# A Fourier filter with two MLPs on one core: the third matrix's sums, loads, spare buffers and output stores are re-timed

## The chip, the core and the metric

The kernel runs on one core of one Trainium2 chip. The metric is device time in microseconds (us) of one execution; times are compared by the median of several executions. TensorE (PE) multiplies matrices, VectorE (DVE) and ScalarE (ACT) work on tiles element by element, GpSimd (POOL) does a little arithmetic and issues the accumulating transfers, SyncE (SP) issues most other transfers. Each engine runs its instructions in order and waits on semaphores of the others.

## The reference

The input is two batches of 3008 tokens by 256 features. It is filtered along the tokens in the frequency domain, and the 6016 tokens then go through two MLPs, all in float32:

```
X = np.fft.rfft(x, axis=1)
y = np.fft.irfft(X * (filt_r + 1j * filt_i)[None], n=3008, axis=1)   # 2 x 3008 x 256
h = y.reshape(6016, 256) @ w_in              # 256 -> 2048
x2 = (h * sigmoid(h)) @ w_out                # 2048 -> 256
g = x2 @ w_gate                              # 256 -> 1536
out = (g * sigmoid(g) * (x2 @ w_val)) @ w_out2   # 1536 -> 256
```

## The kernel before

The filter is a prime-factor transform of 64 by 47 points done with matrix products. Numbers are split in a high and a low part, both of a type that TensorE takes, and a product of two such operands is three matmuls (high by high, high by low, low by high). Where "operand" stands below, making one means a copy by ScalarE that rounds to the high part and a subtraction by VectorE that leaves the low part.

Three stages follow one another on TensorE: the filter, the first MLP (its last blocks as `Wide` units) and the second MLP, from about 604 us to the end. Only that last stage and its seam with the stage before matter here. It works on 6 blocks of up to 1024 tokens (`STEP2`), 6 units of `Pair` per block, 36 in all. A unit computes a part of gate and value (`Gate`, g and v) by a scheme with 7 products of quarter blocks in the place of 8, so 14 products or 42 matmuls, and leaves SiLU(g) times v in two tiles: ga (L1026, with both quarters of one row of the scheme) and c.

**Gate and value on the side engines.** In a unit ScalarE copies banks of sums on (L876, L879, L894) and applies SiLU (L1027, L1031, L1037, L1039), VectorE adds banks (L903, L909) and multiplies by the values (L1045, L1049, L999, L1008). TensorE's next products wait for L876, L894 and L909, which put back into PSUM what it goes on accumulating.

**The third matrix** (w_out2) is multiplied by the same scheme on pairs of units: 17 "chains" (`CHAINS`) of two units each, 3 per block, with the last unit pair done by 16 plain products (`product8`). The chains run beside the units on the same engines. `Pair.run` calls `tick()` (L1208) seven times; each tick may queue one product of three matmuls (`product7`), which TensorE then does between those of gate and value. The clock starts at tick −19, and a chain takes 14 ticks: seven operands k in the order 3, 1, 7, 5, 2, 6, 4 (`ORDER7`), each for its pair-halves p = 0 and 1 (the two units). Around a chain's tick 0 stand, by tables of tick numbers:

- `high7` (L1097) and `lower7` (L1102) make operand k, so many ticks ahead of its product (`EARLY`).
- `more` (L1086 to 1090) makes the sums that some operands are, in place: `SUMS` names the tick, the target k and the addend j. The first, (1, 7), adds two quarters in ga, to be operand 5; (1, 3) and (7, 3) add a quarter of c to ga, (4, 6) one of ga to c. A sum is a transfer of POOL's queue that adds as it writes (L1088), 256 KB; in the first and the last two chains the first sum is VectorE's (L1090).
- `load7` (L1108 to 1111) has SP load the third matrix's parts in four pieces, up to 512 KB each, into tiles w7 of the pool `late["p"]`, 9 buffers that ga, w7 and the input differences xr share in turn.
- `after7` (L1123, L1125, L1136, L1142) adds the products' banks into oa, and `store2` turns an oa tile (L1250) and writes it out by 4 strided transfers per quarter on SP (L1253).

**What is in between.** `side(k)` runs what a table (`todo2`, filled by `later`) holds for a step of a unit: the loads of gate and value weights (`load_s2`), the next block's input x2 (`load_x2`), its differences on POOL (`prep_x2`, L809) and its operands xo (`split_x2`; L796 on ScalarE, L799 on VectorE). `split_op` can put the low half on a list `lag` for later. The order of every engine is that of the program text; buffers of a pool are handed out in turn, and a tile waits until its buffer's last reader is done.

**The seam.** In the first MLP's last block ScalarE copies four x2 tiles from the sums (L748) and issues their stores itself (L750). The spare pool here called sp has 2 buffers of the tag s, for `Gate.s` of the `Wide` units and `done7` of the chains; the pool tp has 4 of the tag u.

Of the kernel before, what the change touches and what calls it, by code (L numbers as in the profile page):

```python
# [11 lines left out]
F32 = mybir.dt.float32  # L12
# [17 lines left out]
P = 128  # L30
# [3 lines left out]
STEP2 = 1024  # L34
# [85 lines left out]
def fft_filter_mlp_kernel(  # L120
# [609 lines left out]
    def wide_out(b, f, h):  # L730
# [5 lines left out]
        def one(m, l, k):  # L736
# [9 lines left out]
            if end and k == 1:  # L746
                u = tp.tile([P, 512], F32, tag="u", name="x2")
                nc.scalar.copy(u[:, :n], a)  # L748
                eng = nc.scalar if b == len(WIDE) - 1 else nc.sync
                eng.dma_start(d3[NSTD + 2 * b + l][:, m, :n], u[:, :n])  # L750
# [56 lines left out]
    def prep_x2(t, part):  # L807
# [6 lines left out]
        if t:  # L814
            r = late["p"].tile([P, 2, 512], F32, tag="mid", name="xr")
        else:
            r = mid([P, 2, 512], "xr")
# [267 lines left out]
    def more(c, k, j, p):  # L1085
        o, v = view(c, k, p), view(c, j, p)  # L1086
        if (k, j) != (1, 7) or 0 < c < CHAINS - 2:
# [4 lines left out]
    SUMS = ((-5, 1, 7), (1, 1, 3), (4, 7, 3), (8, 4, 6))  # L1092

    def high7(c, k, p):
        x = ops7[c, k, p] = mid([P, 2, 512], "ho", F32R)
# [69 lines left out]
    for p, first in ((0, (-9, -8, -7, -6)), (1, (-4, -3, -2, -1))):  # L1165
# [24 lines left out]
    def product8(p, v, l, m, i):  # L1190
# [10 lines left out]
        if end and i == 2:  # L1201
            a = turned[t, m][:, l, :n]
            nc.vector.tensor_tensor(a, o, a, op=ALU.add)
            if l == 1:
                turned["o", m] = mid([P, 2, 512], "ob")
            store2_part(t, m, l, turned[t, m], turned["o", m], (nc.sync, nc.scalar))

    def tick():  # L1208
# [13 lines left out]
        for k in ORDER7:  # L1222
            at7 = where(i + EARLY[k] - 1, k)
            if at7:
                lower7(*at7)
        for k in ORDER7:
            at7 = where(i + EARLY[k], k)
            if at7:
                high7(*at7)
        for o, k, j in SUMS:  # L1230
            c, r = divmod(i - o, 14)
            if r < 2 and 0 <= c < CHAINS:
                more(c, k, j, r)
        for r, o in enumerate((-4, 3, 9, 21)):
# [6 lines left out]
    def store2(t, m):  # L1241

        o = mid([P, 2, 512], "ob")
        a = turned.pop((t, m))
        for l in range(2):
            store2_part(t, m, l, a, o)

    def store2_part(t, m, l, a, o, engines=(nc.sync,)):
        n = size2(t) // 2
        nc.vector.transpose(o[:, l, :n], a[:, l, :n])  # L1250
        r0 = STEP2 * t + n * l
        for i in range(4):
            engines[i % len(engines)].dma_start(  # L1253
                out[r0:r0 + n, P * m + 32 * i:P * m + 32 * i + 32].rearrange("(j r) c -> r j c", r=32),
                o[32 * i:32 * i + 32, l, :n].rearrange("p (j c) -> p j c", c=32),
# [105 lines left out]
    for u in range(6 * NBLK2):  # L1361
        later(u, 0, load_s2, u + 1, "g")
# [3 lines left out]
    for t in range(1, NBLK2):  # L1366
        for m in range(2):
            later(6 * t + 3 + 2 * m, 2 - m, store2, t - 1, m)
# [3 lines left out]
        for k, n in ((0, 1), (1, 5), (3, 6)):  # L1372
            later(u + 4, k, split_x2, t, n)
# [278 lines left out]
```

## Time and profile before

| what | value |
|---|---|
| median of 3 executions | 1156.52 us (1152.58 to 1157.79) |
| the profiled execution | 1157.94 us, its span 1156.2 us |
| mean granted clock of TensorE | 0.989 |
| TensorE, VectorE, ScalarE, POOL busy | 97%, 72%, 67%, 35% |
| TensorE's share of the chain of waits | 82% (transfers 6%, VectorE 5%, ScalarE 5%) |
| DMA | 215.62 MB, 48.4% of 16 engines' time by the hardware queues, 17.2% by POOL's |

The span is what the profiler saw between the first and the last instruction; the execution's own time is 1.74 us longer, and the median of the three is 1.42 us shorter than this execution. "Busy" is a share of the whole span. The profile names lines of the kernel: L843 is the matmul of gate and value (and of all second-matrix-like products), L1150 that of a chain. A matmul of 128 by 512 starts some 0.23 us after the one before where nothing is in its way.

### The profile page before, as it was taken

To read this page: it belongs to the slowest core of one execution; us is meant where nothing else is said; L and a number is where in the kernel's file an instruction comes from. 1 tells how busy PE (TensorE), PEld (TensorE's weight loads), DVE (VectorE), ACT (ScalarE), POOL (GpSimd) and SP (SyncE) were. 2 spreads that over 40 slices of the span, in tenths; PEclk is the share of its full clock that TensorE was granted. 3 is DMA by queue.
4 is the path that set the end of the run, shared out by engine and by line. 5 is a ranking of instruction groups with operands and counts; after the bars stand their busy time and mean duration, and the time that the engine had idled before them with its cause. 6 is when DMAs were issued, how large, how long until landed. Compare 5 with 4: busy or idle time off the path is not lost.

```text
span 1156.2 us, 15345 instructions
## 1 busy us (share of the span) xinstructions
PE 1116.5 (97%) x4999; PEld 917.0 (79%) x4999; DVE 835.4 (72%) x1297; ACT 774.0 (67%) x1461; POOL 407.8 (35%) x382
## 2 busy tenths in 40 slices
PE   9999999999999999999999999999998999998996
PEld 7588888998888887888877788778777777877886
DVE  5987365666676786776646788787796786876885
ACT  5788766766677686686556776666675676675671
POOL 3557735554513542632102333222322322322120
PEclk9999999999999999999999999999998999998998
DMA  8974543337355356435446788798899789789794
GB/s 240 287 239 110 158 134 113 128 116 227 109 178 169 136 195 212 147 134 195 170 173 204 157 222 233 172 266 237 191 218 232 166 216 270 165 210 236 180 234 82
DMA packets 148815, 215.62 MB, mean 186 GB/s; under 512 B 58880, under 2 KB 87936, under 8 KB 148736
## 3 DMA queue, kind: packets, MB, share of 16 engines
q1 hardware_dynamic: 125280, 179.26, 48.4%
q0 software_dynamic: 18720, 33.69, 17.2%
q10 hardware_dynamic: 4736, 1.70, 0.6%
q8 instruction: 39, 0.64, 0.2%
q14 instruction: 40, 0.33, 0.1%
HBM read 138.20 MB, written 42.73 MB: 156 GB/s over the span
## 4 chain that ended last, share of the span: by engine, by line
PE 82%; DMA 6%; DVE 5%; ACT 5%; issue 2%; SPq 0%; ACTq 0%; DVEq 0%
PE bk L843 21%; PE acc L742 15%; PE bk L1150 11%; PE acc L719 7%; PE h L669 7%; PE y L843 6%; DMA ga<-ga 4%; PE xb L843 4%; PE xa L843 4%; PE s L209 2%; PE s L397 2%; PE s L206 2%; DMA w<-d 1%; PE s L282 1%; ACT ho L1097 1%
## 5 line engine op out<-in xcount | busy, mean ns | idle before, releaser
L843 PE MATMUL bk<-xo,wst 128*128 128x512 f32 (+1 forms) x864 | 281.6, 391 | 20.1 <-ACT bk L876 15.1
L742 PE MATMUL acc<-h,w 128*128 128x512 f32 x768 | 283.6, 389 | 0.0
L1150 PE MATMUL bk<-ho,w 128*128 128x512 f32 (+1 forms) x714 | 269.1, 394 | 0.2 <-DMA w<-d 0.2
L843 PE MATMUL bk<-xo,w 128*128 128x512 f32 (+1 forms) x648 | 211.1, 392 | 7.7 <-DVE c L909 7.2
L843 PEld LDWEIGHTS bk<-xo,wst 128*128 128x128 f32 x864 | 163.4, 190 | 58.5 <-ACT bk L876 19.2
L742 PEld LDWEIGHTS acc<-h,w 128*128 128x128 f32 x768 | 144.2, 188 | 29.6
L1150 PEld LDWEIGHTS bk<-ho,w 128*128 128x128 f32 x714 | 137.3, 192 | 25.2 <-DMA w<-d 0.5
L843 PEld LDWEIGHTS bk<-xo,w 128*128 128x128 f32 x648 | 121.2, 189 | 39.4 <-DVE c L909 15.9
L1088 POOL DMA_DIRECT2D ga<-c x68 | 59.5, 1086 | 244.7 <-DVE ho L1102 210.1
L1097 ACT CAST ho<-ga 128x512 fp32r<-128x512 f32 (+1 forms) x136 | 82.6, 619 | 30.1 <-DMA ga<-ga 28.6
L1102 DVE TENSOR_TENSOR ho<-ga,ho 128x512 fp32r<-128x512 f32 (+1 forms) x136 | 90.8, 675 | 8.4 <-ACT ho L1097 8.4
L719 PE MATMUL acc<-h,w 128*128 128x512 f32 (+1 forms) x384 | 95.4, 376 | 0.0
L669 PE MATMUL h<-xh,w 128*128 128x512 f32 (+1 forms) x248 | 83.6, 379 | 0.0
L719 PEld LDWEIGHTS acc<-h,w 128*128 128x128 f32 x384 | 71.2, 188 | 11.2
L1102 DVE TENSOR_TENSOR ho<-c,ho 128x512 fp32r<-128x512 f32 (+1 forms) x102 | 77.1, 758 | 1.4 <-ACT ho L1097 1.4
L677 DVE TENSOR_TENSOR h<-h,h 128x512 fp32r<-128x512 f32 (+1 forms) x64 | 41.4, 654 | 48.3 <-ACT h L676 46.9
L843 PE MATMUL xb<-xo,wst 128*128 128x512 f32 x192 | 74.7, 391 | 1.6 <-DVE h L936 1.6
L843 PE MATMUL xa<-xo,w 128*128 128x512 f32 x192 | 75.3, 394 | 0.0
L843 PE MATMUL y<-xo,wst 128*128 128x512 f32 x192 | 74.7, 389 | 0.0
L876 ACT COPY bk<-bk 128x512 f32<-128x512 f32 (+1 forms) x72 | 41.2, 572 | 48.7 <-PE bk L843 24.8
L903 DVE TENSOR_TENSOR bk<-bk,u 128x512 f32<-128x512 f32 (+1 forms) x72 | 49.2, 684 | 27.5 <-PE bk L843 23.2
L1088 POOL DMA_DIRECT2D ga<-ga x28 | 24.1, 860 | 114.0 <-DVE ho L1102 55.1
(161 smaller groups left out, 2208.9 us busy)
## 6 DMA issues: line engine op xcount, KB each, us to landing
w<-d SPq DMA_DIRECT2D x53, 512.0 KB, 6.9
wst<-ds_g SPq DMA_DIRECT2D x36, 512.0 KB, 5.7
wst<-ds_v SPq DMA_DIRECT2D x36, 512.0 KB, 5.3
wst<-ds SPq DMA_DIRECT2D x32, 512.0 KB, 4.6
ga<-c POOLq DMA_DIRECT2D x60, 256.0 KB, 4.6
c<-ga POOLq DMA_DIRECT2D x30, 256.0 KB, 5.7
ga<-ga POOLq DMA_DIRECT2D x28, 256.0 KB, 7.6
zt<-d SPq DMA_DIRECT2D x16, 384.0 KB, 4.7
```

What stands on the lines that cost most here:

```text
L206: nc.tensor.matmul(o, cst[:k, c:c + n], x, start=True, stop=True)
L669: nc.tensor.matmul(ps[:, :n], wt[key, f // 4, g][:, wpart, o:o + P], x[xpart][:, g, :n], start=(g == 0 and k == 0), stop=(g == 1 and k == 2),)
L677: nc.vector.tensor_tensor(h[:, 1, :n], u[:, :n], h[:, 0, :n], op=ALU.subtract)
L719: nc.tensor.matmul(a[:, :n], w[:, wpart, o:o + 128], h[:, xpart, :n], start=(f == 0 and k == 0), stop=(f == 15 and k == 2),)
L742: nc.tensor.matmul(a, w[:, wpart, o:o + 128], h[xpart][:, n * l:n * l + n], start=(f == 0 and k == 0), stop=(end and k == 1), skip_group_c ...
L843: nc.tensor.matmul(o, w(wpart), x[:, xpart, :o.shape[-1]], start=(first and k == 0), stop=(last and k == 2), skip_group_check=True,)
L876: nc.scalar.copy(self.y, self.a)
L903: nc.vector.tensor_tensor(self.b, self.b, self.u2, op=ALU.add)
L1088: nc.gpsimd.dma_start(o, v, accum_op=ALU.add)
L1097: nc.scalar.copy(x[:, 0, :v.shape[-1]], v)
L1102: nc.vector.tensor_tensor(x[:, 1, :n], v, x[:, 0, :n], op=ALU.subtract)
L1150: nc.tensor.matmul(o, w7[c, k][:, p, wpart], ops7[c, k, p][:, xpart, :n], start=(k in (1, 5) and p == 0 and i == 0), stop=(k in (2, 3, 4) ...
```

## The change

Seven edits. TensorE's matmuls and their order stay as they are.

1. In the first MLP's last block two of the four x2 copies go to VectorE, and all four stores to POOL's queue.
2. The input differences of `prep_x2` go into a spare buffer of sp (tag s) in place of one of `late["p"]` (of `mid` for the first block).
3. The first sum: pair-half 0 by POOL's transfer at tick −7 (from −5), pair-half 1 always by VectorE at tick −4. `SUMS` now has a tick for each pair-half. Operand 1's copy of pair-half 0 is made 3 ticks sooner, into a tile of `late["p"]`.
4. The first load of a chain at tick −2 (from −4), the gate weights' load one side step later.
5. The last block's extra operands (`HIGH8`) at ticks −4 to −1 and 2 to 5 after chain 16 (from −9 to −6 and −4 to −1).
6. `store2` by quarters, at four places of a block where two halves stood; the turned tile is from tp.
7. The low halves of the next block's operands are put off to the next `side()` call, and `prep_x2`'s second part comes one step later.

```diff
--- before.py
+++ after.py
@@ -745,8 +745,8 @@
             )
             if end and k == 1:
                 u = tp.tile([P, 512], F32, tag="u", name="x2")
-                nc.scalar.copy(u[:, :n], a)
-                eng = nc.scalar if b == len(WIDE) - 1 else nc.sync
+                (nc.vector.tensor_copy if m and b == len(WIDE) - 1 else nc.scalar.copy)(u[:, :n], a)
+                eng = nc.gpsimd if b == len(WIDE) - 1 else nc.sync
                 eng.dma_start(d3[NSTD + 2 * b + l][:, m, :n], u[:, :n])
 
         queue.extend((one, m, l, k) for m in range(2) for k in (0, 2) for l in range(2))
@@ -811,10 +811,7 @@
             x[4] = x[2]
             sub(x[4], x[2], x[6])
             return
-        if t:
-            r = late["p"].tile([P, 2, 512], F32, tag="mid", name="xr")
-        else:
-            r = mid([P, 2, 512], "xr")
+        r = sp.tile([P, 2, STEP2 // 2], F32, name="s")
         x[5], x[6], x[7] = x["b12"], r[:, 1, :n], r[:, 0, :n]
         sub(x[7], x[3], x["b12"])
         sub(x[5], x["b12"], x[1])
@@ -1084,15 +1081,19 @@
 
     def more(c, k, j, p):
         o, v = view(c, k, p), view(c, j, p)
-        if (k, j) != (1, 7) or 0 < c < CHAINS - 2:
+        if (k, j, p) != (1, 7, 1):
             nc.gpsimd.dma_start(o, v, accum_op=ALU.add)
         else:
             nc.vector.tensor_tensor(o, o, v, op=ALU.add)
 
-    SUMS = ((-5, 1, 7), (1, 1, 3), (4, 7, 3), (8, 4, 6))
+    SUMS = (((-7, -4), 1, 7), ((1, 2), 1, 3), ((4, 5), 7, 3), ((8, 9), 4, 6))
 
     def high7(c, k, p):
-        x = ops7[c, k, p] = mid([P, 2, 512], "ho", F32R)
+        if (k, p) == (1, 0):
+            x = late["p"].tile([P, 2, 512], F32R, tag="mid", name="ho")
+        else:
+            x = mid([P, 2, 512], "ho", F32R)
+        ops7[c, k, p] = x
         v = view(c, k, p)
         nc.scalar.copy(x[:, 0, :v.shape[-1]], v)
 
@@ -1162,7 +1163,7 @@
             for m in range(2):
                 AT8[T0 + first[2 * x + m]] = p, v, l, m
     HIGH8 = {}
-    for p, first in ((0, (-9, -8, -7, -6)), (1, (-4, -3, -2, -1))):
+    for p, first in ((0, (-4, -3, -2, -1)), (1, (2, 3, 4, 5))):
         for x, (v, l) in enumerate(((0, 0), (0, 1), (1, 1), (1, 0))):
             HIGH8[T0 + first[x]] = p, v, l
 
@@ -1201,9 +1202,7 @@
         if end and i == 2:
             a = turned[t, m][:, l, :n]
             nc.vector.tensor_tensor(a, o, a, op=ALU.add)
-            if l == 1:
-                turned["o", m] = mid([P, 2, 512], "ob")
-            store2_part(t, m, l, turned[t, m], turned["o", m], (nc.sync, nc.scalar))
+            store2(t, m, l, (nc.sync, nc.scalar))
 
     def tick():
         i = clock[0]
@@ -1219,40 +1218,34 @@
         at7 = where(i)
         if at7:
             queue.extend((product7, *at7, k) for k in range(3))
-        for k in ORDER7:
-            at7 = where(i + EARLY[k] - 1, k)
-            if at7:
-                lower7(*at7)
-        for k in ORDER7:
-            at7 = where(i + EARLY[k], k)
-            if at7:
-                high7(*at7)
-        for o, k, j in SUMS:
-            c, r = divmod(i - o, 14)
-            if r < 2 and 0 <= c < CHAINS:
-                more(c, k, j, r)
-        for r, o in enumerate((-4, 3, 9, 21)):
+        for d, fn in ((1, lower7), (0, high7)):
+            for k in ORDER7:
+                for p in range(2):
+                    at7 = where(i + EARLY[k] + 3 * (k == 1 and p == 0) - d, k)
+                    if at7 and at7[2] == p:
+                        fn(*at7)
+        for when, k, j in SUMS:
+            for p in range(2):
+                c, r = divmod(i - when[p], 14)
+                if r == 0 and 0 <= c < CHAINS:
+                    more(c, k, j, p)
+        for r, o in enumerate((-2, 3, 9, 21)):
             c, x = divmod(i - o, 14)
             if x == 0 and 0 <= c < CHAINS:
                 load7(c, r)
 
     turned = {}
 
-    def store2(t, m):
-
-        o = mid([P, 2, 512], "ob")
-        a = turned.pop((t, m))
-        for l in range(2):
-            store2_part(t, m, l, a, o)
-
-    def store2_part(t, m, l, a, o, engines=(nc.sync,)):
+    def store2(t, m, l, engines=(nc.sync,)):
+
         n = size2(t) // 2
-        nc.vector.transpose(o[:, l, :n], a[:, l, :n])
+        o = tp.tile([P, 512], F32, tag="u", name="ob")
+        nc.vector.transpose(o[:, :n], turned[t, m][:, l, :n])
         r0 = STEP2 * t + n * l
         for i in range(4):
             engines[i % len(engines)].dma_start(
                 out[r0:r0 + n, P * m + 32 * i:P * m + 32 * i + 32].rearrange("(j r) c -> r j c", r=32),
-                o[32 * i:32 * i + 32, l, :n].rearrange("p (j c) -> p j c", c=32),
+                o[32 * i:32 * i + 32, :n].rearrange("p (j c) -> p j c", c=32),
             )
 
 
@@ -1359,24 +1352,24 @@
         for n, args in enumerate((("g", q), ("v", q), ("a22", q))):
             later(2 * q - 2, n, load_2, *args)
     for u in range(6 * NBLK2):
-        later(u, 0, load_s2, u + 1, "g")
+        later(u, 1, load_s2, u + 1, "g")
         later(u, 3, load_s2, u + 1, "v")
     later(0, -1, split_x2, 0, 7)
     later(0, 0, split_x2, 0, 4)
     for t in range(1, NBLK2):
-        for m in range(2):
-            later(6 * t + 3 + 2 * m, 2 - m, store2, t - 1, m)
+        for n, k, m, l in ((3, 2, 0, 0), (4, 0, 0, 1), (4, 2, 1, 1), (5, 0, 1, 0)):
+            later(6 * t + n, k, store2, t - 1, m, l)
         u = 6 * t - 6
         later(u + 2, 0, load_x2, t)
         later(u + 3, 1, prep_x2, t, 0)
         for k, n in ((0, 1), (1, 5), (3, 6)):
-            later(u + 4, k, split_x2, t, n)
+            later(u + 4, k, split_x2, t, n, True)
 
         for k, n in ((1, 2), (4, 3)):
-            later(u + 5, k, split_x2, t, n)
-        later(u + 5, 2, prep_x2, t, 1)
-        later(u + 6, -1, split_x2, t, 7)
-        later(u + 6, 0, split_x2, t, 4)
+            later(u + 5, k, split_x2, t, n, True)
+        later(u + 5, 3, prep_x2, t, 1)
+        later(u + 6, -1, split_x2, t, 7, True)
+        later(u + 6, 0, split_x2, t, 4, True)
 
 
     F0, F1 = Fft(0), Fft(1)
@@ -1598,6 +1591,9 @@
         for u in range(6 * NBLK2):
 
             def side(k):
+                now, lag[:] = lag[:], []
+                for fn in now:
+                    fn()
                 for fn, args in todo2.pop((u, k), ()):
                     fn(*args)
```

The changed file is shorter by 3 lines from L818 on; L1097 becomes L1098, L1102 L1103, L1111 L1112, L1150 L1151, and of the lines above the chains L876 becomes L873, L894 L891, L903 L900, L909 L906, L1027 L1024, L1031 L1028, L1088 L1085, L1090 L1087, L1250 L1243, L1253 L1246.

On POOL, two chains of the second block. ga<-ga is a first sum, c<-ga the (4, 6) sum, ga<-c the sums with a quarter of c; L809 works on the next block's differences. Before:

```order
L1088 DMA c<-ga 128x512
L1088 DMA ga<-ga 128x512
L1088 DMA c<-ga 128x512
L1088 DMA ga<-ga 128x512
L1088 DMA ga<-c 128x512 x4
L809 TENSOR_TENSOR x_5781<-x_5781,xr 128x512
```

And in the changed kernel:

```order
L1085 DMA ga<-ga 128x512
L1085 DMA c<-ga 128x512 x2
L1085 DMA ga<-c 128x512 x4
L809 TENSOR_TENSOR x_5779<-x_5779,s 128x512
L1085 DMA ga<-ga 128x512
L1085 DMA c<-ga 128x512 x2
```

One first sum per chain is left on POOL, and it stands ahead of both (4, 6) sums of the chain before.

On VectorE, the place in the first block where the next block's operands are made (L799; xo<-x and xo<-xr, later xo<-s). Before:

```order
L903 TENSOR_TENSOR bk<-bk,u_5997 128x512
L1102 TENSOR_TENSOR ho<-c,ho 128x512
L909 TENSOR_TENSOR c<-bk,s_5977 128x512
L799 TENSOR_TENSOR xo<-x_5780,xo 128x512
L1102 TENSOR_TENSOR ho<-c,ho 128x512
L1102 TENSOR_TENSOR ho<-ga,ho 128x512
L799 TENSOR_TENSOR xo<-xr,xo 128x512
L1045 SCALAR_TENSOR_TENSOR ga<-bk,ga 128x512
L1102 TENSOR_TENSOR ho<-ga,ho 128x512
L903 TENSOR_TENSOR bk<-bk,u_6062 128x512
L1049 TENSOR_TENSOR ga<-bk,ga 128x512
L909 TENSOR_TENSOR c<-bk,s_6049 128x512
```

And in the changed kernel:

```order
L1087 TENSOR_TENSOR ga<-ga 128x512
L900 TENSOR_TENSOR bk<-bk,u_5997 128x512
L1103 TENSOR_TENSOR ho<-c,ho 128x512
L906 TENSOR_TENSOR c<-bk,s_5979 128x512
...
L900 TENSOR_TENSOR bk<-bk,u_6062 128x512
L1046 TENSOR_TENSOR ga<-bk,ga 128x512
L906 TENSOR_TENSOR c<-bk,s_6048 128x512
L996 SCALAR_TENSOR_TENSOR c<-c 128x512
L1103 TENSOR_TENSOR ho<-ga,ho 128x512
L799 TENSOR_TENSOR xo<-s,xo 128x512
```

The low half xo<-xr stood ahead of the sums L903 and L909 of its step; xo<-s stands behind them. The row L1087 is an added first sum of pair-half 1.

On SP, the loads of a chain in the second block (w_ is a w7 tile, wst gate or value weights). Before:

```order
L1111 DMA w_6531<-d_0_109 128x1024
L648 DMA wst<-ds_v_103 128x1024
L648 DMA wst<-ds_g_98 128x1024
L1111 DMA w_6651<-d_0_109 128x1024
L1253 DMA out_dram<-ob 32x16x32 x8
```

And in the changed kernel:

```order
L648 DMA wst<-ds_g_97 128x1024
L1112 DMA w_6556<-d_0_109 128x1024
L648 DMA wst<-ds_v_103 128x1024
L1112 DMA w_6649<-d_0_109 128x1024
L648 DMA wst<-ds_g_98 128x1024
L1246 DMA out_dram<-ob 32x16x32 x4
```

The chain's first load (from d_0) keeps its neighbours and is released two ticks later; the output goes four strips at a time.

## Rows read from the trace of the kernel before

**Rows 1.** The page, first part: busy us, share of the span, instructions

```profile
PE 1116.5 (97%) x4999; PEld 917.0 (79%) x4999; DVE 835.4 (72%) x1297; ACT 774.0 (67%) x1461; POOL 407.8 (35%) x382
```

**Rows 2.** TensorE's waits from 603 us on: total us, times, longest us

```profile
PE bk L843 <- ACT bk L876: 15.1, 10, 3.5
PE bk L843 <- DVE c L909: 7.2, 6, 2.0
PE bk L843 <- ACT ga L1027: 2.7, 4, 0.7
PE bk L843 <- ACT u L894: 2.3, 1, 2.3
```

**Rows 3.** TensorE's timeline: start us, us, what; in brackets the idle time ahead

```profile
779.09 0.50 PE L843 MATMUL bk<-xo,wst 128*128 128x512 f32 x1 [2.12 <-ACT bk L876]
...
872.20 0.80 PE L843 MATMUL bk<-xo,wst 128*128 128x512 f32 x1 [3.40 <-ACT bk L876]
...
966.58 0.80 PE L843 MATMUL bk<-xo,wst 128*128 128x512 f32 x1 [2.06 <-ACT bk L876]
...
1060.30 0.74 PE L843 MATMUL bk<-xo,wst 128*128 128x448 f32 x1 [3.55 <-ACT bk L876]
...
1128.91 0.68 PE L843 MATMUL bk<-xo,w 128*128 128x448 f32 x2 [1.98 <-DVE c L909]
```

**Rows 4.** ScalarE's timeline at 773 to 782 us

```profile
777.94 0.62 ACT L1097 CAST ho<-ga 128x512 fp32r<-128x512 f32 x1 [3.74 <-DMA ga<-ga]
778.46 0.58 ACT L876 COPY bk<-bk 128x512 f32<-128x512 f32 x1
```

**Rows 5.** The chain of waits from 590 us on: start us, us, what

```profile
767.52 10.40 DMA ga<-ga
...
859.33 11.68 DMA ga<-ga
...
955.07 10.34 DMA ga<-ga
```

**Rows 6.** Groups by line from 603 us on, ScalarE: busy us, mean ns, idle before

```profile
L1097 ACT CAST ho<-ga 128x512 fp32r<-128x512 f32 (+1 forms) x136 | 82.6, 619 | 30.1 <-DMA ga<-ga 28.6 <-DMA ga<-c 1.3
```

**Rows 7.** Timelines of ScalarE and VectorE at 734 to 747 us

```profile
735.71 0.60 ACT L1027 ACTIVATE ga<-bk 128x512 f32<-128x512 f32 x1 [1.97 <-PE bk L1150]
...
742.39 0.69 DVE L799 TENSOR_TENSOR xo<-xr,xo 128x512 fp32r<-128x512 f32 x1 [2.64 <-ACT xo L796]
```

**Rows 8.** Windows: us, busy of PE, PEld, DVE, ACT, POOL, PE's clock, DMA, GB/s

```profile
850.00:900.00 50.00, 46.60 (x193) 37.73 (x193) 35.60 (x58) 30.16 (x57) 9.57 (x11) 0.93 0.94 235
950.00:975.00 25.00, 22.94 (x94) 18.31 (x93) 17.74 (x29) 15.41 (x30) 6.30 (x8) 0.93 1.01 262
1025.00:1050.00 25.00, 23.97 (x108) 19.60 (x107) 23.97 (x40) 17.31 (x34) 8.39 (x9) 1.00 0.86 206
1050.00:1075.00 25.00, 21.45 (x90) 18.44 (x89) 14.56 (x25) 13.29 (x27) 5.21 (x6) 0.86 0.90 234
```

**Rows 9.** Groups by line from 603 us on, VectorE's first sums

```profile
L1090 DVE TENSOR_TENSOR ga<-ga 128x448 f32<-128x448 f32 (+1 forms) x6 | 3.9, 647 | 0.2
```

**Rows 10.** ScalarE's timeline at the stage's opening

```profile
603.82 0.58 ACT L748 COPY x<-acc 128x512 f32<-128x512 f32 x1 [0.45 <-ACT x L748]
604.44 0.33 ACTq L750 DMA_DIRECT2D d<-x  x1
```

**Rows 11.** The page, DMA issues: queue, count, KB each, median us to landing

```profile
w<-d SPq DMA_DIRECT2D x53, 512.0 KB, 6.9
...
ga<-c POOLq DMA_DIRECT2D x60, 256.0 KB, 4.6
...
ga<-ga POOLq DMA_DIRECT2D x28, 256.0 KB, 7.6
```

**Rows 12.** DMA issues at 732.6 to 733.2 us

```profile
w<-d SPq DMA_DIRECT2D x1, 512.0 KB, 11.6
```

## The prediction

> **What bounds the kernel now.** I began with the page: TensorE is busy 1116.5 us of the span, 97% [rows 1]. The reader should see that only what makes TensorE wait, or slows its clock, can be won. The change leaves TensorE's own instructions and their order as they are, so the question is which of its waits go and which come.
>
> Second, the waits of TensorE from 603 us on, the stage that the change rearranges: 15.1 us on ScalarE's copies at L876 (10 waits), 7.2 on VectorE's sums at L909 (6), 2.7 on ScalarE's L1027 (4), 2.3 on L894 (1) [rows 2], 27.3 us together. Third, TensorE's timeline, to place them. The four longest waits on L876 are 2.12, 3.40, 2.06 and 3.55 us, ending at 779.09, 872.20, 966.58 and 1060.30 us [rows 3], one per block of the stage: 11.13 us. That leaves 4.0 us of L876's; and 1.98 of L909's is one wait near the end, at 1128.91 [rows 3].
>
> *Why the four long ones.* ScalarE reached its copy L1097 of a first sum at 774.2 us and stood still 3.74 us until a transfer ga<-ga was in at 777.94; L876, which TensorE needed, is the next instruction on ScalarE and came at 778.46 [rows 4]. In the chain of waits that transfer runs from 767.52 for 10.40 us, and its fellows in the other blocks take 10.34 to 11.68 us (four rows, the shortest and longest shown) [rows 5]. Over the stage ScalarE idles 28.6 us for ga<-ga at L1097, and 1.3 us for ga<-c [rows 6].
>
> *Why the rest.* At 735.71 ScalarE's L1027 has waited 1.97 us for TensorE's third-matrix product L1150: its new tile takes a buffer of which a product still reads weights. ScalarE is then late with its copies, and VectorE idles 2.64 us for ScalarE's xo before L799, an operand's low half, with L909 queued behind it [rows 7]. Such a group stands in each of four blocks; it and two waits at the stage's opening make up 4.0 + (7.2 − 1.98) + 2.7 = 11.9 us of TensorE's waits [rows 2, 3].
>
> The low clock is the last item. The granted clock is 0.93 over 850 to 900 us, 0.93 over 950 to 975 and 0.86 over 1050 to 1075 [rows 8], 1.00 being 2.4 GHz and the lower level, 1.2 GHz, half of it. Lost at most: 0.07 × 50 + 0.07 × 25 + 0.14 × 25 = 8.75 us. Where the clock is already low in the last part of a wait this counts time twice, so I take 6.
>
> **The change, part by part.** A tick of the third matrix's clock is 9 matmuls (42 of the second matrix and 21 of the third in a unit of 7 ticks). An undisturbed 25 us holds 108 matmuls [rows 8], so a matmul is 0.23 us and a tick 2.1.
>
> *First sums.* Pair-half p=1 moves from POOL's transfers to VectorE; p=0 stays a transfer, two ticks (4.2 us) sooner. With 28 transfers before and 17 now, POOL issues 11 fewer. The p=1 copy has no transfer left to wait for. For p=0: in the case at 777.94 TensorE ran dry at 779.09 − 2.12 = 776.97, 9.4 us after the issue at 767.52 [rows 3, 5]. With two ticks more that is 13.6 us, against 10.34 to 11.68 for the worst sums [rows 5]. Gain: 11.1 us of waits and 6 of clock, **17.1**. Price: 11 adds more on VectorE, of 0.647 us by L1090 [rows 9], 7.1 us of busy time. They stand where VectorE idles for TensorE or ScalarE, so I book nothing; without that cover they cost up to 7.1, since VectorE is busy 23.97 of 25 us in the fullest window [rows 8].
>
> *Buffers and low halves.* The input differences leave the pool of the w7 tiles for a spare one, and operand 1's first copy goes into that pool 3 ticks sooner. In the changed order L1027 (now L1024) waits for no weights that a recent product reads, and L799 is put off by one step, behind what TensorE waits for. Both causes of the 11.9 us are taken away; I keep back 0.9 for places where ScalarE is just in time. Gain **11**. The price of the shared spare pool: the last two units of the first matrix get their s tile only when VectorE is done with the old one. I bound this by nothing and, for each, by the 0.7 us that L1027's late buffer cost TensorE at the most [rows 2]; a VectorE instruction more or less decides it, so I take 0.2 for each, 0.4.
>
> *Last block.* Its extra operands come 5 to 6 ticks later, so two of VectorE's low halves no longer stand ahead of L909. The sum after TensorE's product must still be made before TensorE goes on (two VectorE instructions, about 1.1 us). Of 1.98, gain **0.9**.
>
> *Start.* ScalarE loses two copies of 0.58 and four issues of 0.33 us [rows 10] ahead of L894, for which TensorE waits 2.3 us [rows 2]. But L894's tile then waits for a store that POOL issues. Between −0.5 and +1.5 I take **+0.4**, near the low end: ScalarE's row shows what it is freed of, while the store is as long as before. The Trainium skill ("DMA: Bandwidth & Descriptors", Specifications) gives a transfer from the gpsimd queue about 1 us to its first byte, one from the sync or scalar queue about 0.6. By that the store is 0.4 us later, this gain is nil and the total below is 0.4 less; no row of this kernel shows a store by POOL.
>
> *The rest.* Output by quarters issues the same DMAs and transposes in four places instead of two: nothing, hidden on SP and VectorE; uncovered it would be a transpose's 0.68 us per place. The gate weights' load one step later: nothing, several ticks ahead of use. The first third-matrix load goes from tick −4 to −2. Counted in the two orders, 73 to 80 matmuls lay between its release and first use, now 41: 9.4 us. Landing takes 6.9 us in the median [rows 11], 11.6 for one in a crowded stretch [rows 12]. Nothing waits at the median; an 11.6 would cost 2.2. I book **1.6** for new waits on loads and on sums ga<-c, whose lead of about 10 us is unchanged.
>
> Sum: 17.1 + 11 + 0.9 + 0.4 − 0.4 − 1.6 = 27.4. From the profiled execution's 1157.94 us that is 1130.5. It stood 1.4 above the median of 1156.52, so I put the time at **1130** and not at 1129.
>
> **The rivals.**
> - *Loads too late* (the slower side). Place: each chain's first product L1150, waiting for w7. Price: landing less 9.4 us, and about half as much again in clock (6 for 11.1 above), for 17 chains. To be slower by 0.5% it must return 27.4 + 5.8 = 33 us, which is 33 / 17 / 1.5 = 1.3 us of waiting per chain: it decides from a usual landing of 10.7 us on. At 11.6 it would give 1130 + 17 × 2.2 × 1.5 = about 1186. For: the one of 11.6. Against: 6.9 in the median and 11 transfers fewer. Chance 0.04.
> - *The wait moves on.* DMA engines are at 1.01 of their time in 950 to 975 us [rows 8]; if p=0's sums or ga<-c land late instead, half of the 17 stays: 1138.5. For: ScalarE waits 1.3 us for ga<-c already [rows 6]. Against: ga<-c lands in 4.6 us in the median, ga<-ga in 7.6 [rows 11]. Chance 0.12. The Trainium skill (the same page, "Anatomy of one DMA") has a software-queue transfer take 2.0 us and bytes over 436 GB/s, an estimate of 2.6 us for 256 KB. By it there would be no such rival, and no long wait before either; the rows say 7.6 and up to 11.68, and decide.
> - *VectorE becomes the limit.* The 11 adds uncovered, and put-off low halves late for their products: 7.1 and some 2: 1139. Chance 0.11.
> - *It doesn't do what it says.* L1027 waits for products as before: 11 less gain, 1141. Only if the pool hands out its buffers otherwise than in the order. Chance 0.06.
> - *Nothing to speak of*: several of these at once, within 0.5%. Chance 0.07.
>
> **How the numbers follow.** The forecast, within about 6 us of 1130, has 0.60. If every wait above and the clock went, the time would be 1157.94 − 27.3 − 8.75 = 1122, and that is the low end. The high end takes in the three middling rivals and, at half, the unbooked price of 7.1: 1141 + 3 = 1144. A measurement tells this kernel from no change at about 0.5%, 5.8 us, so faster means under 1150.7. Forecast and the three middling rivals lie there: 0.89. Same 0.07, slower 0.04.
>
> **What would show it.** Right: no ga<-ga behind L1098's idle time, PE's clock at 1.00 from 725 to 1100 us, no wait of TensorE on ScalarE's L873 over 1 us, L1024 without idle time for L1150. Wrong: waits of L1150 for w<-d, of L1098 for ga<-c, or of TensorE on VectorE's L906 in every block.

## The result, and the profile after

The changed kernel took 1145.88 us (median of 5; before 1157.73), a ratio of 0.9905 [0.9881, 0.9929]: faster, by some 11 us where 27 were forecast, and 1.9 us outside the range. In one of the five executions TensorE's matmuls took more than twice their usual time throughout (816 ns at L840 against 389, at a granted clock of 1.00), and it was the profiled one; so the profile below is of the first experiment, the same kernel measured again: 1145.98, ratio 0.9911 [0.9888, 0.9934], the profiled execution 1146.67 us.

TensorE's waits in it, from 595 us on (total us, times, longest us), beside [rows 2]:

```profile
PE bk L840 <- ACT u L891: 5.2, 1, 5.2
PE bk L840 <- DMA wst<-ds_g: 4.4, 4, 1.3
PE bk L840 <- DVE c L906: 2.9, 3, 1.5
PE bk L840 <- ACT bk L873: 2.2, 6, 0.8
...
PE bk L1151 <- DMA w<-d: 1.0, 2, 0.6
PE bk L840 <- DMA wst<-ds_v: 0.5, 1, 0.5
```

Of the 15.1 us on L876 2.2 are left on L873, of the 7.2 on L909 2.9 on L906, and L1027's are gone. What is new is the first two rows: one wait of 5.2 us at the stage's opening, and four for gate weights. Windows (columns as in [rows 8]):

```profile
600.00:625.00 25.00, 19.69 (x73) 15.21 (x72) 10.82 (x16) 10.35 (x20) 3.29 (x5) 0.86 0.44 148
850.00:900.00 50.00, 49.10 (x214) 39.51 (x213) 41.84 (x66) 32.35 (x62) 10.36 (x11) 1.00 0.90 246
950.00:975.00 25.00, 24.90 (x110) 19.99 (x109) 20.81 (x35) 16.77 (x33) 6.13 (x7) 1.00 0.89 230
1050.00:1075.00 25.00, 25.00 (x120) 22.11 (x119) 19.46 (x34) 16.81 (x34) 6.12 (x7) 1.00 0.88 222
```

The low clock of [rows 8] is gone; it is now at the opening (0.86), where it was 1.00. ScalarE's groups by line show both causes of the old waits removed:

```profile
L1098 ACT CAST ho<-ga 128x512 fp32r<-128x512 f32 (+1 forms) x136 | 83.0, 621 | 5.2 <-PE bk L840 5.2
...
L1024 ACT ACTIVATE ga<-bk 128x512 f32<-128x512 f32 (+1 forms) x35 | 20.7, 592 | 0.6
```

L1098 idles for no transfer (28.6 us for ga<-ga in [rows 6]), L1024 for no product (1.97 us a time in [rows 7]). All four signs that the prediction named for "right" are there. So the large gain is there and something else gave part of it back. Set matmul against matmul (their order is the same), the 2800th starts at 614.28 us before and 620.97 after: 6.7 us lost by then. From there to the last one, 18.1 are won.

**Where it was lost: the opening.** Timeline of all engines there, before the late matmul:

```profile
602.08 1.84 POOL L750 DMA_DIRECT2D d<-x  x3 [21.55 <-ACT x L748]
...
605.98 0.69 DVE L748 COPY x<-acc 128x512 f32<-128x512 f32 x1 [3.20 <-DMA d<-x]
...
608.63 0.59 ACT L891 COPY u<-bk 128x512 f32<-128x512 f32 x1 [5.88 <-DMA d<-x]
...
609.27 1.65 PE L840 MATMUL bk<-xo,wst 128*128 128x512 f32 x3 [5.19 <-ACT u L891]
```

L891 is ready at 602.75 and stands still 5.88 us until POOL's second store has landed and frees its tile. Landing of these stores, median us, of the first three of four by POOL's queue in the changed kernel, and of the first two of four by ScalarE's before:

```profile
d<-x POOLq DMA_DIRECT2D x3, 256.0 KB, 5.7
```

```profile
d<-x ACTq DMA_DIRECT2D x2, 256.0 KB, 2.0
```

The second store, whose landing decides here, took 5.73 us by POOL and 2.03 by ScalarE. ScalarE's third and fourth took 3.7 and 4.1 and POOL's fourth 2.8, so the queue is not all that sets this time; what else does was not tried.

The size of this loss differs between executions. In e2_load0 and e3_prep (below), whose stores, copies and tiles there are the same, the second store took 4.2 and 4.5 us, TensorE waited 3.7 and 3.9, and the 2800th matmul came 3.8 us later than before, not 6.7.

**Where else: the weights.** SP's timeline in the second block:

```profile
755.05 2.56 SPq L1246 DMA_DIRECT2D out_dram<-ob  x4
757.79 1.38 SPq L1112 DMA_DIRECT2D w<-d  x1
759.22 1.53 SPq L648 DMA_DIRECT2D wst<-ds_g  x1
```

The load of gate weights now stands behind a quarter's four output strips and a w7 load. The strips start right behind VectorE's transpose, which ends at 755.03. The gate weights' load was issued at 749.24 before; now at 759.22, in a program that is 4.4 us later there, and TensorE waits for it 1.04 us, until 766.13.

### The profile page after: what moved, and what is told of

It is laid out like the page before. It is cut to its first block, busy times and chain, and to the rows that moved or that the text cites. A ratio compares the mean times of both kernels' runs of the same rounds, so it can differ in the third digit from the quotient of the medians.

```text
span 2877.7 us, 15370 instructions
## 1 busy us (share of the span) xinstructions
PE 2870.0 (100%) x4999; PEld 1747.0 (61%) x4999; DVE 845.5 (29%) x1310; ACT 795.7 (28%) x1459; POOL 386.6 (13%) x375
## 4 chain that ended last, share of the span: by engine, by line
PE 100%; DVE 0%; issue 0%
PE bk L840 31%; PE acc L742 16%; PE bk L1151 15%; PE acc L719 7%; PE h L669 7%; PE y L840 6%; PE xa L840 4%; PE xb L840 4%; PE s L206 2%; PE s L397 2%; PE s L209 2%; PE s L282 1%; PE bk L1198 1%; PE turn L299 0%; PE h L689 0%; PE warm L191 0%
## 5 line engine op out<-in xcount | busy, mean ns | idle before, releaser
L840 PE MATMUL bk<-xo,wst 128*128 128x512 f32 (+1 forms) x864 | 625.0, 816 | 0.0
L742 PE MATMUL acc<-h,w 128*128 128x512 f32 x768 | 613.9, 828 | 0.0
L1151 PE MATMUL bk<-ho,w 128*128 128x512 f32 (+1 forms) x714 | 568.0, 819 | 0.0
L840 PE MATMUL bk<-xo,w 128*128 128x512 f32 (+1 forms) x648 | 466.4, 815 | 1.2 <-DVE c L906 1.2
L840 PEld LDWEIGHTS bk<-xo,wst 128*128 128x128 f32 x864 | 302.6, 350 | 203.9 <-issue 189.7
L742 PEld LDWEIGHTS acc<-h,w 128*128 128x128 f32 x768 | 271.0, 353 | 184.6 <-issue 183.8
L1151 PEld LDWEIGHTS bk<-ho,w 128*128 128x128 f32 x714 | 251.0, 352 | 161.9 <-issue 160.3
L840 PEld LDWEIGHTS bk<-xo,w 128*128 128x128 f32 x648 | 230.0, 355 | 153.1 <-issue 146.1
L719 PE MATMUL acc<-h,w 128*128 128x512 f32 (+1 forms) x384 | 233.6, 790 | 0.0
L719 PEld LDWEIGHTS acc<-h,w 128*128 128x128 f32 x384 | 135.2, 353 | 78.6 <-issue 77.8
L669 PE MATMUL h<-xh,w 128*128 128x512 f32 (+1 forms) x248 | 182.8, 796 | 0.0
L1085 POOL DMA_DIRECT2D ga<-c x68 | 59.4, 1066 | 816.5 <-DVE ho L1103 770.6
L840 PE MATMUL xa<-xo,w 128*128 128x512 f32 x192 | 160.6, 839 | 0.0
L840 PE MATMUL y<-xo,wst 128*128 128x512 f32 x192 | 158.9, 828 | 0.0
L840 PE MATMUL xb<-xo,wst 128*128 128x512 f32 x192 | 158.2, 826 | 0.0
L873 ACT COPY bk<-bk 128x512 f32<-128x512 f32 (+1 forms) x72 | 40.5, 563 | 291.0 <-PE bk L840 291.0
L900 DVE TENSOR_TENSOR bk<-bk,u 128x512 f32<-128x512 f32 (+1 forms) x72 | 49.6, 689 | 230.1 <-PE bk L840 228.5
L913 DVE TENSOR_TENSOR y<-y,s 128x512 f32<-128x512 f32 x32 | 22.4, 700 | 283.3 <-PE y L840 283.3
```

The source lines that it names most:

```text
L669: nc.tensor.matmul(ps[:, :n], wt[key, f // 4, g][:, wpart, o:o + P], x[xpart][:, g, :n], start=(g == 0 and k == 0), stop=(g == 1 and k == 2),)
L719: nc.tensor.matmul(a[:, :n], w[:, wpart, o:o + 128], h[:, xpart, :n], start=(f == 0 and k == 0), stop=(f == 15 and k == 2),)
L742: nc.tensor.matmul(a, w[:, wpart, o:o + 128], h[xpart][:, n * l:n * l + n], start=(f == 0 and k == 0), stop=(end and k == 1), skip_group_c ...
L840: nc.tensor.matmul(o, w(wpart), x[:, xpart, :o.shape[-1]], start=(first and k == 0), stop=(last and k == 2), skip_group_check=True,)
L873: nc.scalar.copy(self.y, self.a)
L900: nc.vector.tensor_tensor(self.b, self.b, self.u2, op=ALU.add)
```

## The experiments

Eighteen runs. All but three are variants of the changed kernel; where lines were added above, L840, L906, L1098, L1103 and L1151 read L847, L913, L1105, L1110 and L1158 there. Times are medians; each ratio is to the kernel before, measured alongside. The runs stand on five chips in six groups; the median of the kernel before was 1155.3 to 1159.4 us in them (both ends on one chip), so a few us between medians of different groups say little by themselves.

| run | kernel | us | ratio |
|---|---|---|---|
| a0_again | the changed kernel | 1146.0 | 0.9911 [0.9888, 0.9934] |
| e1_start | its opening undone | 1149.1 | 0.9920 [0.9894, 0.9945] |
| s1_actq | only its stores back on ScalarE's queue | 1147.1 | 0.9928 [0.9906, 0.9950] |
| e2_load0 | gate weights' load at its old step | 1141.3 | 0.9858 [0.9837, 0.9879] |
| e3_prep | POOL's difference at its old step | 1147.4 | 0.9915 [0.9890, 0.9939] |
| e4_three | these three undone | 1143.5 | 0.9876 [0.9853, 0.9899] |
| s4_mid | x2 copies in other buffers | 1143.2 | 0.9884 [0.9848, 0.9921] |
| s5_mid_load0 | s4_mid with e2_load0 | 1137.2 | 0.9808 [0.9782, 0.9835] |
| s6_load3 | s5, first load at tick −3 | 1138.6 | 0.9821 [0.9795, 0.9846] |
| s7_half | s5, output by halves | 1149.3 | 0.9906 [0.9872, 0.9939] |
| s8_nolag | s5, no low half put off | 1144.5 | 0.9901 [0.9868, 0.9935] |
| s9_two | s5, operand 2's low half not put off | **1134.4** | 0.9809 [0.9776, 0.9842] |
| s10_dve | s5, that difference by VectorE | 1136.3 | 0.9829 [0.9794, 0.9864] |
| s13_two3 | s9, first load at tick −3 | 1135.5 | 0.9829 [0.9800, 0.9857] |
| s11_pad | s1 with four tiny writes by POOL | 1167.5 | 1.0105 [1.0074, 1.0137] |
| p1_sums | before, with first sums changed | 1144.9 | 0.9903 [0.9870, 0.9936] |
| p2_spare | before, with the spare buffer | 1154.5 | 0.9984 [0.9962, 1.0005] |
| p12 | before, with both | 1143.3 | 0.9892 [0.9851, 0.9932] |

**The same again.** 

> The changed kernel unaltered, for a profile at the usual clock (in the first one TensorE ran at well under half of its usual pace throughout). Theory of the prediction: TensorE's waits from 604 us on add up to under 5 us and ScalarE's idle time at L1098 for ga<-ga is gone; then the missing 15 us lie outside that stage. Rival (loads too late): TensorE's L1151 waits for w<-d, about 1 us in each of the 17 chains. Rival (the wait moves on): ScalarE's L1098 idles some 10 us or more for ga<-c or ga<-ga, and TensorE waits for L873 behind it. Rival (VectorE): TensorE waits for L906 in every block, 5 to 10 us together.

Measured: the rows above. The waits have neither the place of "loads too late" (1.0 us on w<-d in all) nor of the other two rivals; the opening and the gate weights were in no theory.

**The opening.** Three ways to change it:

```diff
-  (nc.vector.tensor_copy if m and b == len(WIDE) - 1 else nc.scalar.copy)(u[:, :n], a)
-  eng = nc.gpsimd if b == len(WIDE) - 1 else nc.sync
+  nc.scalar.copy(u[:, :n], a)                            # e1_start: both lines
+  eng = nc.scalar if b == len(WIDE) - 1 else nc.sync     # s1_actq: this line alone
```

```diff
-  u = tp.tile([P, 512], F32, tag="u", name="x2")         # s4_mid, last block only
+  if l == 0:
+      wide_x2[m] = mid([P, 2, 512], "x2o")
+  u = wide_x2[m][:, l]
```

> The changed kernel with edit 1 undone: all four x2 copies by ScalarE, their stores issued by ScalarE. Theory 1 (POOL's stores land late and hold the tile of L891, which cost 5.2 us of TensorE's waiting and a half clock after it): TensorE's wait on L891 is back at about 2.3 us, the clock over 600 to 625 us at 1.00, and the time 6 to 7 us under the changed kernel, about 1139. Rival (the seam is late for another reason, the other edits have loaded the engines there): under 2 us gained.

> The changed kernel with only the stores of the four x2 tiles back on ScalarE's queue; two copies stay on VectorE. Theory 1 (the store by POOL lands late, and the tile of L891 waits for it): TensorE's wait on L891 falls from 5.2 us to about 2, the first matmul after it starts 3 us sooner. Rival (the copies by VectorE make it late): the wait stays over 4 us. The whole time may move by a few us more either way, as it did when the whole edit was undone and later loads landed otherwise.

> The changed kernel with the four x2 copies of the last block in two tiles of the large pool in place of the four buffers that L891's tile comes from; stores still by POOL. Theory 1: L891 has no store to wait for, TensorE's wait there falls from 5.2 us to under 1, and the time by 4 to 7 us, to 1139 to 1142. Rival (the next thing is late there, the copies or the sums before them): the wait falls to 2 to 3 us only.

The wait on L891 fell from 5.19 us to these, in e1_start and in s1_actq:

```profile
PE bk L840 <- ACT u L891: 2.3, 1, 2.3
PE bk L840 <- ACT u L891: 1.6, 1, 1.6
```

So it is the stores and not VectorE's copies. In s4_mid, where POOL's stores land as late (5.7 us) but no tile waits for them, it is gone, and the 2800th matmul starts 8.3 us sooner than in a0_again. So theory 1 holds for the place. For the time it doesn't: e1_start is not faster, and its clock over 600 to 625 us is 0.93, not the 1.00 expected. Other waits of TensorE in e1_start:

```profile
PE bk L1151 <- DMA w<-d: 6.5, 5, 3.8
PE bk L840 <- DMA wst<-ds_g: 3.8, 3, 2.2
PE bk L840 <- DVE c L996: 2.2, 1, 2.2
```

The last row is a wait for gate weights too: their load landed at 852.67 us, and TensorE went on at 852.81. At the 2800th matmul e1_start is 4.4 us ahead of a0_again, at the 3600th 4.3, at the 4200th no longer: between the last two stand two waits of 2.2 us for gate weights (0.8 and 1.2 in a0_again) and a clock of 0.93 over 850 to 875 us. One wait of 3.8 us for w<-d from 1120 us on (3.6 in s1_actq, 0.6 in a0_again) then puts it behind. In s4_mid, of the 8.3 us, 4.0 are left at the last matmul and 2.8 by medians (1143.2, over the 1139 to 1142 expected), while the gate weights take 6.4 us in the place of 4.4:

```profile
PE bk L847 <- DMA wst<-ds_g: 6.4, 4, 2.5
```

**The gate weights.** `later(u, 0, load_s2, u + 1, "g")` in the place of step 1.

> The changed kernel with the gate weights' load back at the side step before, ahead of the output's last quarter on SP. Theory 2 (SP's order makes that load late, by the 4.4 us of TensorE's waits on wst<-ds_g and about as much in weight loads that start late): those waits are gone, 1140 to 1142. Rival (the transfers' engines are full and the next wait ends at the same time, on VectorE's L906 or on w<-d): 1145 to 1146.

> The changed kernel with the x2 copies of the last block in the large pool and the gate weights' load back at its old step. If the seam (some 6 to 8 us) and the load's place (5) are the two mis-sized terms and their costs add up: 1133 to 1136. If the time at the seam is given back by later transfers, as in the kernel with the stores on ScalarE's queue: 1138 to 1141.

No wait on wst<-ds_g is left in either. From s4_mid to s5_mid_load0, with the same opening, the load alone is worth 6.0 us (6.2 at the last matmul of the profiles). e2_load0 agrees, but not by its distance to a0_again: of the 5.5 us at the last matmul 2.9 are there at the 2800th already. Its partner is e3_prep, on the same chip, whose edit moved nothing (next part) and whose 2800th matmul starts within 0.02 us of its own: there the load is worth 5.5 us at the last matmul, 6.1 by medians. e3_prep, for its part, is 2.9 us ahead of a0_again at the 2800th matmul and level with it at the last (1136.86 and 1136.85 us): with the gate weights late, what the opening wins is not kept. The two terms together bring 1146.0 to 1137.2. s5_mid_load0's waits are short:

```profile
PE bk L1158 <- DMA w<-d: 4.1, 8, 1.1
PE bk L847 <- DVE c L913: 3.7, 6, 1.5
PE bk L847 <- ACT bk L880: 2.0, 5, 0.8
```

**POOL against VectorE.** In the changed kernel TensorE waits 1.26 us on L906 at 677.71, which it did not before. Its timeline ahead of that wait:

```profile
671.54 0.68 DVE L1103 TENSOR_TENSOR ho<-ga,ho 128x512 fp32r<-128x512 f32 x1
671.77 1.61 POOL L809 TENSOR_TENSOR x<-x,s 128x512 f32<-128x512 f32 x1 [4.16 <-DVE xo L799]
...
672.15 1.78 DVE L1103 TENSOR_TENSOR ho<-c,ho 128x512 fp32r<-128x512 f32 x1
```

A low half of two operands takes 1.78 us in the place of 0.68 while POOL's difference runs. VectorE has no pause from there to L906 at 676.98, which comes 1.1 us later for it. The put-off low half L799 is what releases POOL.

> The changed kernel with the second part of the input differences (POOL's L809) back at its step of before. Theory 3 (in every block a low half L1103 of VectorE that starts during POOL's L809 lasts 1.8 us in the place of 0.7, and L906 behind it is late): TensorE's 1.26 us wait on L906 near 676 us is gone, 1144 to 1145; in the later blocks the late weights still decide. Rival (the wait comes of the put-off low halves, not of POOL): no change, the wait stays.

> The same kernel with the low half of operand 2 alone not put off, and POOL's last difference, which waits for it, a step sooner. If the two engines' meeting place decides: POOL's L809 meets another low half, with slack behind it, the 1.27 us wait goes, 1135 to 1137. If not: the wait stays, 1137 to 1139.

> The kernel with the seam's copies in the large pool and the gate weights' load at its old step (1137.2), and the last of the input differences made by VectorE in the place of POOL. If VectorE is held by POOL's L809 (the low half L1103 that starts 0.4 us after it lasts 1.8 us in the place of 0.7) and this makes L906 late by the 1.27 us at 668 and some 0.4 in the later blocks: these waits go, 1134.5 to 1136. If the put-off low halves alone make L906 late: VectorE has 0.6 us more to do there, the wait stays and the time is the same or 1 to 3 us more.

In e3_prep POOL still waited for the put-off L799: nothing moved, and the expectation was misconceived. With operand 2's low half not put off (`split_x2` with `n != 2` for its last argument, `prep_x2` a step sooner) L809 runs at 661.19 and the next low halves last 0.69 us:

```profile
661.19 1.52 POOL L816 TENSOR_TENSOR x<-x,s 128x512 f32<-128x512 f32 x1 [1.82 <-DVE xo L806]
...
662.72 0.68 DVE L1110 TENSOR_TENSOR ho<-ga,ho 128x512 fp32r<-128x512 f32 x1
```

The 1.27 us wait is gone and the time 1134.4: 2.8 us under s5_mid_load0 by medians, 2.2 at the last matmul of the two profiles, though the ratio is the same, as the kernel before was faster beside it too. With the difference on VectorE no low half there lasts over 0.7 us; the wait shrinks to 0.77 us, as VectorE now has the difference's 0.68 us to do, and the time is 1.8 us over s9_two's. So the held low half and its wait are shown; its price in the whole time is at the edge of what can be told, and s9_two also has one put-off low half fewer.

**All three undone.** 

> All three of these in one kernel. If theories 1 to 3 hold and their gains add up: 1133 to 1136, near the 1130 of the prediction, with TensorE's waits from 600 us on at some 7 us. If the gains are of one wait that the others uncover: 1137 to 1139.

At 1143.5 it is above both ranges. It had the late wait of e1_start (3.6 us for w<-d, from 1113.7), so the sum was not to be seen in it.

**Each old cause by itself, on the kernel before.** The edits are those of `more` and of `prep_x2` in the diff above.

> The kernel before, and of the change only this: the first sum of pair-half 1 always by VectorE, of pair-half 0 always by POOL's transfer, at the ticks of before. Theory of the prediction: the four long waits on L876 (11.1 us) and the low clock (some 6) go, but not the waits on L1027 and L909: 1139 to 1142. Rival (the wait moves to the sum of pair-half 0 or to ga<-c): 1147 to 1151.

> The kernel before, and of the change only the input differences in a spare buffer of the pool sp. Theory of the prediction: ScalarE's L1027 no longer waits for L1150, the four groups of three waits (9.8 us) go in the main, the four long waits stay: 1147 to 1149. Rival (without that late start the transfers ga<-ga are only waited for longer): 1153 to 1157.

> The kernel before with two parts of the change together: first sums of pair-half 1 by VectorE (1144.9 alone) and input differences in the spare pool (1154.5 alone). If the late buffer's cost was only hidden behind the long waits in the second: L1027's and L876's waits of some 1.4 us per block are gone, 1139 to 1141. If the spare pool costs as much elsewhere: 1143 to 1146.

p1_sums alone has the whole net gain of the change: the four long waits and the low clock are gone (0.997 in the mean), though pair-half 0 keeps its old tick; ScalarE's idle time at L1097 for ga<-ga falls from 28.6 to 2.9 us. Its waits on L909 grew from 7.2 us to:

```profile
PE bk L843 <- DVE c L909: 11.4, 12, 2.0
```

That is the price of the added work on VectorE, six new waits of 0.64 to 0.81 us, and with it the time is 3 us over the range expected. In p2_spare the waits on L1027 are gone and the four long ones, 11.1 us before, add up to 14.0 (3.35, 3.03, 3.54, 4.04): what comes sooner waits longer for the transfer, as the rival had it. (Its profiled execution was 7 us over its median.) With both, 1.6 us less than p1_sums, within the uncertainty; the 1139 to 1141 of the theory did not come.

**The last edits, on s5_mid_load0.** Output by halves is `((3, 2, 0, 0), (3, 2, 0, 1), (5, 1, 1, 0), (5, 1, 1, 1))` in the loop over `store2`.

> The same kernel with no low half put off (the whole last edit undone). Theory of the prediction: the waits of 1.0 to 1.1 us on L906 in each block and the two at the stage's opening come back, 6 to 8 us more, 1143 to 1145. Rival (putting off only exchanges them for the 1.27 us wait and its like): 1136 to 1139.

> The same kernel as the first of these with the output by halves at the places of before, 8 strips at a time. If the quarters' places on SP matter (a load behind a store that waits for VectorE's transpose): 2 to 4 us more or less, by whether the loads stand behind 8 strips or behind 4. If only the bytes count: the same within 1.5 us.

> That kernel with a chain's first load one tick sooner (tick -3). If TensorE's waits on w<-d (2 to 5 us in the runs so far) come of the 9.4 us that the load now has: 2 to 4 us under it. If the transfer engines are full there: the same time, the wait on the weights of gate and value instead.

> The fastest kernel so far (1134.4) with a chain's first load at tick -3 as well. If its 5.1 us of waits on w<-d are the lead of that load: 1131 to 1133. If the time is limited by the transfers as a whole, as with the tick alone: 1134 to 1136.

Putting low halves off is worth 7.3 us by medians, 9.5 at the last matmul: without it L913's waits come back (7.8 us, 8 times), as expected. Halves cost 12 us (14.1 at the last matmul), far over the expectation, in two places, and the mean clock falls from 0.997 to 0.993:

```profile
PE bk L847 <- DVE c L913: 7.8, 12, 1.5
PE bk L847 <- DMA wst<-ds_v: 5.0, 4, 1.6
```

Two transposes in a row delay L913 by 0.94 to 1.01 us a block, and value weights wait behind eight strips. The tick of the first load is worth nothing: with one tick more the waits on w<-d fall (4.1 to 2.1 us, 5.1 to 3.9) and the time doesn't.

**The wait for w<-d near the end.** In e1_start POOL issues its last four sums ga<-c together at 1107.69, though the low half that the first waits for had ended at 1105.43; in a0_again the first goes at 1104.86. In both an instruction transfer of queue q8 falls between 1105 and 1106 us; POOL has four instructions fewer in e1_start, so its fetch may lie ahead of all four there and behind the first in a0_again. That is a guess; no run shows that a fetch holds a transfer up.

> The kernel with the x2 stores on ScalarE's queue (1147.1, with a wait of 3.6 us on w<-d near 1117 us that the changed kernel does not have), and four tiny writes by POOL where its four stores stood, so that POOL has as many instructions as in the changed kernel. If the wait at 1117 comes of where POOL fetches its instructions (a fetch lies ahead of four sums in a row and makes them 2 to 3 us late): it falls to about 1 us, 1143 to 1145. If it comes of anything else in the exchange of queues: it stays at 3 to 4 us, 1146 to 1148.

This failed as an experiment. With the tiny tile for the writes (4 bytes a partition) TensorE's matmuls became longer: up to the 2750th it lost 4.5 us against s1_actq, 0.43 for each 250 in the first MLP's last part. At the last matmul it is 17 us behind, with long waits for value weights among them (4.5 us), and the time rose by 20 us. POOL's four sums still went together. What makes the wait near 1117 stays open.

## Why the prediction was wrong

*First sums, 17.1: right in mechanism, some us too high.* The four waits and the low clock are gone. p1_sums alone is 14.7 us ahead of the kernel before at the last matmul of the two profiles, 10.3 by medians. "I book nothing" for VectorE's work was wrong by 4 us (six waits of 0.64 to 0.81); in a0_again, with the other edits, none of the six stands. One reading was wrong without harm: the transfers of 10.34 to 11.68 us [rows 5], taken there as the worst that pair-half 0 has to outlast, are pair-half 1's, the second of each pair. Pair-half 0's landed in 8.3 to 8.9 us in the same four places, and in p1_sums they come soon enough at their old tick, so the two ticks more had little to win.

*Buffers and low halves, 11: about right in sum, not in its parts.* I gave both edits the waits by their names. The buffer alone is worth 1 to 2 us, within the uncertainty (p2_spare, p12), since VectorE's L909 is late a few us on in any case; putting low halves off is worth 7 to 10 (on s5_mid_load0).

*The failing step: "Start … I take +0.4 … while the store is as long as before".* POOL's second store lands 5.7 us after its issue where ScalarE's took 2.0, and L891's tile waits for it. The 2.3 us wait became 5.2, with a clock of 0.86 behind it: the 2800th matmul is 6.7 us late (3.8 in e2_load0 and e3_prep), outside the −0.5 to +1.5 that I had for the term. I named the very wait and then gave it no duration. The rule of the Trainium skill ("DMA: Bandwidth & Descriptors", Specifications) pointed the right way, with 0.4 us for 3.7.

*Second: "The gate weights' load one step later: nothing, several ticks ahead of use".* It costs 6.0 us (s4_mid to s5_mid_load0; 5.5 to 6.1 from e2_load0 to e3_prep). The step was counted in ticks, not against what now stands ahead of it on SP: a quarter's strips that wait for VectorE.

*Third, left out altogether:* POOL's difference meets VectorE, some 2 us at the most (2.2 in s9_two's trace, nothing by the ratios). The row was there before: L1102 ho<-c averaged 758 ns, ho<-ga 675.

*Last block, 0.9:* 1.98 became 1.50, so 0.5. *New waits on loads, 1.6:* 1.0 on w<-d and 0.5 on wst<-ds_v, right. The 25 us taken as undisturbed for the 0.23 us of a matmul hold a wait of 0.95; 975 to 1000 us holds 111 matmuls, so 0.225 and 9.2 us for 41 of them, which changes nothing.

With a0_again's opening these add up to 1130.5 + 7.1 (the opening, +0.4 to −6.7) + 6.0 + 2.2 + 0.4 = 1146.2, beside the profiled 1146.67. That it closes so well is partly luck. The opening's 6.7 us are one execution's, the first sums by themselves brought less than the 17.1 that stand in it, and the parts don't add in every order: without the opening's wait the kernel gains 2.8 us by medians while the gate weights are late, 4.1 once they aren't (e2_load0 to s5_mid_load0, 5.5 us apart at the 2800th matmul). Output by quarters, booked at nothing, prevents 12 us in s5_mid_load0.

Of the rivals, none came: loads of w7 cost 1.0 us, transfers ga<-c none, VectorE's limit showed only where POOL held it. The signs of being right or wrong could not have warned either: they stand where the old waits were, and none at the opening or on the weights of gate and value.

## What to carry to other kernels

A tile's wait for a store is a term of its own: take the landing time on the queue that the store moves to, and where that queue shows no such store, bound it by its slowest transfers (here POOL's sums of 4.6 to 11.7 us stood in the rows). A load that moves "a step" moves past what stands in its queue; read there whose result the instruction ahead of it waits for. When a large wait goes, test each edit on the kernel without that wait, as it hides what the others are worth.

## What the runs showed of the hardware

VectorE's low halves of two operands from SBUF were held while POOL computed. At 672.15 one lasts 1.78 us, to 673.93; POOL's L809 ends at 673.38, 0.55 us earlier, and the low half by itself takes 0.68. The Trainium skill ("SBUF — State Buffer", "SBUF: two separate sides") has a port pair that VectorE's instructions with two SBUF inputs and GpSimd's that read SBUF hold for a whole instruction each, the other standing still; the trace agrees, for the fifteen low halves that last over 1 us in this stage all began during an L809. VectorE's sums with one operand in PSUM kept their 0.7 us.

A 128x512 matmul grew from 389 to 391 ns (L742, L744 in s11_pad) when one small tile was put ahead of others in SBUF; which tile's place does it was not tried. The chip isn't the reason: s13_two3, on the same one, has 389.
